# Moving the small transfers of row maxima from SyncE's transfer queue to ScalarE's, in a fused attention and gated-MLP block

## The chip, the cores and the metric

The kernel runs on one core of a Trainium2 chip. The time is that of one execution on the device in microseconds (us), and the median of three runs stands for the kernel. PE is TensorE, DVE is VectorE, ACT is ScalarE, POOL is GpSimd, SP is SyncE, which computes nothing and only starts transfers.

## The reference

S is 2048 rows, D is 512, there are 32 heads of 16 columns, and the gated MLP has 896 columns in each half.

```python
xn = layernorm(x)
q, k, v = split_heads(xn @ wqkv)                    # 32 heads of 16
p = softmax((q @ k.T) * 16 ** -0.5)                 # 2048 x 2048 for each head
attn = merge_heads(p @ v) @ wo
z = gelu(xn @ w_in)                                 # 2048 x 1792
z1, z2 = z[:, :896], layernorm(z[:, 896:])
mlp = (z1 * (w_sp @ z2 + b_sp[:, None])) @ w_out    # w_sp is 2048 x 2048
out = x + attn + mlp
```

## The kernel before

**Attention** sets the beat. Heads are taken in 16 pairs; a pair's queries are cut into 4 blocks of 512, so that there are 64 blocks, numbered here 0 to 63 in the order of work. A block has three kinds of work on PE. *Maxima* (`maxima`, L1237) are 16 steps of two matmuls that form raw scores with the queries on the partitions; DVE reduces each pair of PSUM banks to its row maxima (`max_red`, L826). *Scores* (`scores`, L1223) are 16 steps of two matmuls that form the scores again with the keys on the partitions, less the row's maximum, which takes part as two more rows of the stacked queries `qst` (rows 48 and 49 of 64, hence 50 rows in the profile's shapes). ACT takes the exponential of each step into a tile `pf` (L86, 128x1024). *Values* (`values`, L1324) multiply eight `pf` tiles at a time with the values, twice a block; the first half's sum is copied by ACT into `e`, the second is added to it by DVE (L1346).

**The row maxima have to travel.** They come out with the queries on the partitions and are needed as rows of `qst`. `max_fin` (L837 to L841) folds a block's maxima into `mrow`, one DVE transpose (L843) turns them into `ms`, one transfer *stores* `ms` in a small scratch tensor `mscr` in HBM (16 KB), and two transfers *load* it from there as the two rows of each head of the pair (`qst<-mscr`, 4 KB each). Scores of the block may stand on PE only from the planned time `maxready` on. Maxima are planned up to about 30 steps ahead of scores.

**Everything else is PE filler.** All projections, the spatial matmul `w_sp @ z2`, the output projections (`dense`, L1282) are cut into slots of two matmuls on half the rows each and are laid between the steps of attention by the pattern `ORDER`. Maxima, scores and values share three PSUM tiles `sl` of two banks; the filler has a pair of its own, `dps`. Weights and intermediate results travel by some 1350 transfers; the spatial weights `wsp` are split by POOL (L286 cast, L288 difference), the spatial inputs `zs` are loaded from `z2scr`.

**The order is written at build time by a planner** that keeps a clock for PE (`T["P"]`), ACT (`"A"`), DVE (`"D"`) and POOL (`"G"`). `spawn(generator, priority, ready)` puts a generator on its list; what it yields says on which engine the next piece runs and how long it is planned to take, `("T", us)` is a plain delay. `advance(t)` runs the pieces that are due. `after(us, move, ...)` puts a transfer on a list of times, and `flush()`, called once at each turn of the main loop, issues those that are due on SP's queue in order of time (`move`, L142, is SP's issue). Every queue then works in that order: an instruction that waits holds all that stand behind it on its engine, and no engine knows the planner's times.

**Eight counters.** A transfer from SP's or ACT's queue raises one of eight counters, named DMAHW0 to DMAHW7 in the program, and takes them in turn in the order in which the program was written, whichever of the two queues issues it. Before it may start, the transfer that used the same counter before, which is the eighth one before it, must have landed. That wait stands on the engine that issues the later transfer.

Of the kernel before, what the change touches and what calls it, by code (L numbers as in the profile page):

```python
# [68 lines left out]
def fused_block(ctx, tc, x, wqkv, wo, w_in, w_spT, b_sp, w_out, out):  # L69
    nc = tc.nc  # L70
# [11 lines left out]
    T = {"P": -1000.0, "A": 0.0, "D": 0.0, "G": -1000.0}  # L82
    ends = [0.0]
# [30 lines left out]
    qst = [cp.tile([P, S], F32R, name=f"qst{a}") for a in range(2)]  # L114
# [11 lines left out]
    mscr = [dr.tile([4, 32, 32], F32, name=f"mscr{i}") for i in range(4)]  # L126
# [11 lines left out]
    def raw(t):  # L138
        return t.bitcast(F32) if t.dtype == F32R else t
# [4 lines left out]
    def clock():  # L144
        return T["P"]
# [7 lines left out]
    def at(t, fn, *args):  # L153
        late.append((t, len(late), fn, args))
# [4 lines left out]
    def after(us, fn, *args):  # L159
        at(ends[0] + us, fn, *args)  # L160
# [26 lines left out]
    def queue_up(gen, prio, n, ready):  # L187
        want = next(gen, None)
        if want is not None:
            tasks.append((want[0], want[1], max([ready, *want[2:]]), prio, n, gen))  # L190

    def spawn(gen, prio=2, ready=None):
        count[0] += 1
        ends[0] = clock() if ready is None else ready
        queue_up(gen, prio, count[0], ends[0])
# [623 lines left out]
    maxready = {}  # L819

    def max_red(i, k, ready):
        g, (t, kc) = i // 16, divmod(i % 16, 4)
        yield "D", td(1024)
        if i % 16 == 0:
            mmax[g] = at_.tile([P, 2, 4, 4], F32, tag="mm", name=f"mm{g}", bufs=2)
        nc.vector.tensor_reduce(mmax[g][:, :, t, kc], sl[k], AX.X, ALU.max)  # L826
        free_slot(k)
        if i % 16 == 15:
            yield from max_fin(g)

    def max_fin(g):
        p, c = divmod(g, 4)
        yield "D", 0.95
        mm = mmax.pop(g)
        mn = at_.tile([P, 2, 4, 2], F32, tag="mn", name=f"mn{g}", bufs=1)
        mr = mrow[:, 0:16].rearrange("p (j a t) -> p j a t", j=2, a=2)
        nc.vector.tensor_reduce(mr[:, :, 0, :], mm, AX.X, ALU.max, negate=True)  # L837
        nc.vector.tensor_reduce(mn[:, :, :, 0], mm, AX.X, ALU.max, negate=True)
        nc.vector.tensor_reduce(mn.bitcast(F32R)[:, :, :, 1], mm, AX.X, ALU.max)
        with nc.allow_low_precision(reason="the second of two parts, of which the first is exact"):  # L840
            nc.vector.tensor_reduce(mr[:, :, 1, :], mn, AX.X, ALU.add)  # L841
        ms = at_.tile([P, 32], F32, tag="ms", name=f"ms{g}", bufs=2)
        nc.vector.transpose(ms, mrow.bitcast(F32))  # L843
        after(0.3, move, mscr[g % 4].rearrange("b k x -> (b k) x"), ms)
        for j in range(2):
            row = 64 * j + KS
            after(6.5 if g else 3.3, move, qst[p % 2][row:row + 2, c * 512:(c + 1) * 512].rearrange("a (t b x) -> a t b x", t=4, b=4), mscr[g % 4][:, 8 * j:8 * j + 8, :].rearrange("b (a t) x -> a t b x", a=2))
        maxready[g] = ends[0] + (12.0 if g else 8.5)

    def norm_out(g4, c):  # L850
        nh = 6 if g4 == 3 else 8
# [273 lines left out]
    with tc.manual_schedule(engines=engines):  # L1125
# [50 lines left out]
        stpos = {}  # L1176
        mode = "R"
        spawn(max_fin(0), 0, T["D"])
        n_st, n_mx, n_pv = 0, 16, 0

# [187 lines left out]
        while n_pv < N or queue or tasks or late or urgent or turn or slots:  # L1368
            t = T["P"]
# [74 lines left out]
```

## Time and profile before

| | |
|---|---|
| median of 3 runs | 1839.94 us (1839.93 to 1842.82) |
| the profiled execution, its span | 1837.59 us, 1835.7 us |
| PE, DVE, ACT, POOL busy | 98%, 79%, 66%, 37% of the span |
| granted TensorE clock | 0.998 |
| transfers of SP's queue | 53.0% of the 16 DMA engines' time |

The span is what the trace covers; the execution's own time is 1.9 us longer. A row of the timeline has start, duration, engine, line, operation, what is written and read, the number of instructions merged, and in brackets how long the engine was idle before and what ended that. A transfer's row shows its issue alone, on the queue of the engine that issues it (SPq), not when its data lands; a start is the time at which its waits were over. In the chain of work that ended last, a piece named DMA runs from a transfer's issue until its data landed.

### The profile page before, as it was taken

The page shows a single profiled execution, that of the slowest core. Times are in us where ns is not written, and L with a number is a line of the kernel's source. Part 1 is how long each engine was busy: PE and PEld are TensorE (multiplying, and loading weights), DVE is VectorE, ACT ScalarE, POOL GpSimd, SP SyncE. Part 2 cuts the span into 40 slices and gives each one's busy share as a digit, 9 for nine tenths or more (in the row PEclk, how much of TensorE's full clock was granted, in tenths as well). Part 3 has the DMA queues.
Part 4 walks back from the last instruction along what each step waited for, and adds up shares of the span by engine and source line. Part 5 has one row for each costly group of instructions (what it writes and reads, how often), then busy time and mean ns, then how long its engine had stood idle before and what let it go on. Part 6 is the DMA issues. An engine that isn't in the chain of part 4 may idle for free.

```text
span 1835.7 us, 38100 instructions
## 1 busy us (share of the span) xinstructions
PE 1800.9 (98%) x14744; PEld 1087.7 (59%) x14744; DVE 1443.6 (79%) x1695; ACT 1211.2 (66%) x1329; POOL 684.3 (37%) x786
## 2 busy tenths in 40 slices
PE   9999999999999999999999999999999999999998
PEld 7656566566556565565655655656566665656553
DVE  8858787888887787788877887778778877888882
ACT  4347777888877777566666665666666665666655
POOL 5451141677768677212532244103422140002201
PEclk9999999999999999999999999999999999999999
DMA  7866654433654236647757568655757477466422
GB/s 264 284 234 212 211 187 134 122 113 109 186 185 135 96 99 212 157 137 185 224 154 199 158 189 195 168 143 161 187 150 183 135 210 170 121 155 169 134 89 102
DMA packets 214911, 305.64 MB, mean 166 GB/s; under 512 B 37745, under 2 KB 107953, under 8 KB 214721
## 3 DMA queue, kind: packets, MB, share of 16 engines
q1 hardware_dynamic: 207240, 275.93, 53.0%
q0 software_dynamic: 7488, 27.27, 4.3%
q8 instruction: 116, 1.90, 0.5%
q14 instruction: 67, 0.54, 0.1%
HBM read 193.27 MB, written 109.85 MB: 165 GB/s over the span
## 4 chain that ended last, share of the span: by engine, by line
PE 91%; DVE 4%; DMA 2%; issue 1%; ACT 1%; SPq 1%; POOL 0%; DVEq 0%; POOLq 0%; ACTq 0%
PE dps L1282 36%; PE sl L1324 24%; PE sl L1223 14%; PE sl L1237 12%; DVE mm L826 4%; PE dps L1296 1%; SPq L142 1%; PE sl L247 1%; DMA zs<-z2scr 1%; PE sl L248 1%; PE sl L249 1%; ACT pf L86 0%; PE sl L970 0%; DMA wsp_14r<-in_w_spT 0%; PE sl L1039 0%
## 5 line engine op out<-in xcount | busy, mean ns | idle before, releaser
L826 DVE TENSOR_REDUCE mm<-sl 128x2 f32<-128x1024 f32 x1008 | 1208.7, 1222 | 187.7 <-PE sl L1237 178.8
L86 ACT ACTIVATE pf<-sl 128x1024 f32<-128x1024 f32 x1024 | 1042.9, 1026 | 329.0 <-PE sl L1223 292.4
L1324 PE MATMUL sl<-pf,vall 128*32 128x512 f32 x4096 | 467.9, 595 | 0.7 <-DVE on L960 0.7
L1223 PE MATMUL sl<-qst,kst 50*128 50x512 f32 x2048 | 435.0, 418 | 7.5 <-DVE mm L826 2.3
L1237 PE MATMUL sl<-kst,qst 48*128 48x512 f32 x2016 | 414.8, 404 | 3.9 <-DVE mm L826 2.6
L1282 PE MATMUL dps<-wsp,zs 64*128 64x512 f32 x2352 | 381.0, 392 | 2.2 <-DMA zs<-z2scr 1.4
L1223 PEld LDWEIGHTS sl<-qst,kst 50*128 50x128 f32 x2048 | 194.3, 184 | 221.0 <-issue 80.6
L1324 PEld LDWEIGHTS sl<-pf,vall 128*32 128x32 f32 x4096 | 119.2, 109 | 266.5 <-issue 235.0
L1237 PEld LDWEIGHTS sl<-kst,qst 48*128 48x128 f32 x2016 | 191.8, 185 | 104.5 <-ACT pf L86 49.4
L1282 PEld LDWEIGHTS dps<-wsp,zs 64*128 64x128 f32 x2352 | 227.6, 187 | 38.5 <-DMA zs<-z2scr 2.1
L86 ACT ACTIVATE e<-sl 128x512 f32<-128x512 f32 x64 | 38.3, 598 | 189.8 <-PE sl L1324 175.1
L1346 DVE TENSOR_TENSOR e<-sl,e 128x512 f32<-128x512 f32 x64 | 44.3, 692 | 130.1 <-PE sl L1324 85.5
L729 POOL TENSOR_TENSOR hhl<-z1i,hhl 128x512 fp32r<-128x512 f32 x28 | 35.9, 1292 | 281.1 <-ACT hhl L86 259.1
L1282 PE MATMUL dps<-w,xt 64*128 64x448 f32 x768 | 110.5, 368 | 1.7
L1282 PE MATMUL dps<-wout,hp 64*128 64x512 f32 x672 | 110.5, 392 | 0.1
L877 POOL TENSOR_TENSOR ob<-ob 128x512 f32<-128x512 f32 (+1 forms) x16 | 20.5, 1284 | 169.1 <-DMA ob<-rscr 151.5
L1282 PEld LDWEIGHTS dps<-w,xt 64*128 64x128 f32 x768 | 73.7, 186 | 16.1 <-issue 8.5
L1282 PEld LDWEIGHTS dps<-wout,hp 64*128 64x128 f32 x672 | 64.3, 187 | 10.2 <-issue 0.5
L397 POOL TENSOR_TENSOR qkhl<-qr,qkhl 128x512 fp32r<-128x512 f32 x24 | 30.4, 1284 | 102.3 <-ACT qkhl L86 92.4
L873 POOL TENSOR_TENSOR ob<-ob 128x512 f32<-128x512 f32 (+1 forms) x16 | 20.6, 1287 | 104.2 <-DMA ob<-escr 104.2
L1282 PE MATMUL dps<-wf,zs 64*128 64x512 f32 x336 | 55.6, 393 | 0.1
L1282 PE MATMUL dps<-xnT,wqk 64*128 64x512 f32 x288 | 48.0, 394 | 0.3
(292 smaller groups left out, 1693.1 us busy)
## 6 DMA issues: line engine op xcount, KB each, us to landing
zs<-z2scr SPq DMA_DIRECT2D x192, 256.0 KB
escr<-e SPq DMA_DIRECT2D x60, 256.0 KB
hscr<-hhl POOLq DMA_DIRECT2D x28, 512.0 KB, 6.0
qst<-qscr SPq DMA_DIRECT2D x60, 192.0 KB
kst<-kscr SPq DMA_DIRECT2D x60, 192.0 KB
qscr<-qkhl SPq DMA_DIRECT2D x16, 512.0 KB
kscr<-qkhl SPq DMA_DIRECT2D x16, 512.0 KB
xt<-xscr SPq DMA_DIRECT2D x64, 128.0 KB
```

The source lines that it names most:

```text
L86: return nc.scalar.activation(out, in_, func, **kw)
L142: nc.sync.dma_start(raw(dst), raw(src))
L397: nc.gpsimd.tensor_sub(hl[:, 1, :], raw_, hl[:, 0, :].bitcast(F32))
L729: nc.gpsimd.tensor_sub(hl[:, 1, :], z1, hl[:, 0, :].bitcast(F32))
L826: nc.vector.tensor_reduce(mmax[g][:, :, t, kc], sl[k], AX.X, ALU.max)
L873: nc.gpsimd.tensor_add(both_[rows, 0, :], both_[rows, 0, :], both_[rows, 1, :])
L877: nc.gpsimd.tensor_mul(both_[rows, 0, :], both_[rows, 0, :], both_[rows, 1, :])
L1223: nc.tensor.matmul(sl[k][:, j, :], kst[p % 2][rows, kt * P:(kt + 1) * P], qst[p % 2][rows, c * 512:(c + 1) * 512], start=True, stop=True)
L1237: nc.tensor.matmul(sl[k][:, j, :], qst[p % 2][rows, tt * P:(tt + 1) * P], kst[p % 2][rows, kc * 512:(kc + 1) * 512], start=True, stop=True)
L1282: nc.tensor.matmul(dps[:, bank, :w], lhs, rhs, start=go, stop=stop)
L1324: nc.tensor.matmul(sl[k][cols:cols + VW, 0, :], vpack(kt + r, 2 * p + j), pf[:, j * 512:(j + 1) * 512], start=n % CYC == 0, stop=n % CYC = ...
L1346: nc.vector.tensor_add(e, sl[k][:, 0, :], e)
```

## The change

The store and the two loads of each block go out on ACT's queue (`nc.scalar.dma_start`) in place of SP's, and they are planned otherwise. Before, all three were on the list of times: the store 0.3 us after the folding was planned to end, the loads 6.5 us after it (3.3 us for the first block). Now a new generator, `max_rows`, is spawned with priority 1, that of the exponentials: the store is an ACT piece of 0.15 us, the loads one ACT piece of 0.3 us, planned 4.5 us (2.5 us for the first block) after the store. `maxready` keeps its 12.0 us (8.5 us), counted from 0.1 us later, since `spawn` moves the time it is counted from. No arithmetic changes, and no wait for data: the store still waits for `ms`, the loads for the store's landing.

```diff
         nc.vector.transpose(ms, mrow.bitcast(F32))
-        after(0.3, move, mscr[g % 4].rearrange("b k x -> (b k) x"), ms)
+        spawn(max_rows(p, c, g, ms), 1, ends[0] + 0.1)
+        maxready[g] = ends[0] + (12.0 if g else 8.5)
+
+    def max_rows(p, c, g, ms):
+
+        yield "A", 0.15
+        nc.scalar.dma_start(mscr[g % 4].rearrange("b k x -> (b k) x"), ms)
+        yield "T", 4.5 if g else 2.5
+        yield "A", 0.3
         for j in range(2):
             row = 64 * j + KS
-            after(6.5 if g else 3.3, move, qst[p % 2][row:row + 2, c * 512:(c + 1) * 512].rearrange("a (t b x) -> a t b x", t=4, b=4), mscr[g % 4][:, 8 * j:8 * j + 8, :].rearrange("b (a t) x -> a t b x", a=2))
-        maxready[g] = ends[0] + (12.0 if g else 8.5)
+            nc.scalar.dma_start(raw(qst[p % 2][row:row + 2, c * 512:(c + 1) * 512].rearrange("a (t b x) -> a t b x", t=4, b=4)), mscr[g % 4][:, 8 * j:8 * j + 8, :].rearrange("b (a t) x -> a t b x", a=2))
```

**Where the instructions now stand.** Of the 192 transfers, 64 stores and 128 loads, all leave SP (1349 rows, now 1157) and come to ACT (1312, now 1504). Lines after L843 have numbers 7 higher in the changed kernel. The names in the rows below are tiles with a running number; the brackets name the counters and engines that a row waits for.

The first place is block 31, where the second quarter of the spatial weights is being loaded. SP's queue before:

```order
L142 DMA zs_10446<-z2scr 64x2x512 [waits DMAHW0_49]
L142 DMA mscr_166<-ms_10468 128x32 [waits DMAHW1_49,DVE_49]
L142 DMA wsp_14r<-in_w_spT 128x512 [waits DMAHW4_49,DMAHW2_49,Pool_49]
L142 DMA wsp_15r<-in_w_spT 128x512 [waits DMAHW3_49,PE_49]
L142 DMA qst_91<-mscr_166 2x16x32 [waits DMAHW1_49]
L142 DMA qst_91<-mscr_166 2x16x32 [waits DMAHW5_49]
L142 DMA zs_10586<-z2scr 64x2x512 [waits DMAHW6_49,DMAHW2_49,Pool_49]
L142 DMA zs_10586<-z2scr 64x2x512 [waits DMAHW7_49]
L142 DMA os_3_10492<-escr_3_134 128x1x32 [waits DMAHW0_49]
```

The counters run on by one from row to row, and the two loads stand ahead of the `zs` loads, which wait for POOL. The same place of SP's queue now:

```order
L142 DMA zs_10436<-z2scr 64x2x512 [waits DMAHW0_49]
L142 DMA wsp_14r<-in_w_spT 128x512 [waits DMAHW4_49,DMAHW1_49,Pool_49]
L142 DMA wsp_15r<-in_w_spT 128x512 [waits DMAHW6_49,DMAHW2_49,Pool_49]
L142 DMA zs_10575<-z2scr 64x2x512 [waits DMAHW3_49,DMAHW1_49,Pool_49]
L142 DMA zs_10575<-z2scr 64x2x512 [waits DMAHW5_49]
L142 DMA os_3_10482<-escr_3_134 128x1x32
L142 DMA os_3_10482<-escr_3_134 128x1x32 [waits DMAHW7_49]
L142 DMA ob_3_10483<-escr_3_134 128x1x512 [waits DMAHW0_49]
```

The three small transfers are gone; `wsp_15r` takes counter 2, the first `zs_10575` counter 3, and counter 4, which is skipped here, is the store's. ACT's queue at the same place now:

```order
L86 ACTIVATE pf_10432<-sl_201 128x1024 [waits DVE_49,PE_49]
L850 DMA mscr_166<-ms_10458 128x32 [waits DMAHW4_49,DVE_49]
L86 ACTIVATE e_2_10478<-sl_201 128x512 [waits PE_49]
L86 ACTIVATE pf_10489<-sl_202 128x1024 [waits PE_49,Activation_49]
L86 ACTIVATE pf_10505<-sl_201 128x1024 [waits PE_49,Activation_49]
L855 DMA qst_91<-mscr_166 2x16x32 [waits DMAHW4_49,DMAHW2_49]
L855 DMA qst_91<-mscr_166 2x16x32 [waits DMAHW3_49]
L86 ACTIVATE pf_10524<-sl_203 128x1024 [waits DVE_49,PE_49,Activation_49]
```

The store now stands ahead of the copy to `e`, the loads ahead of the third exponential after it; the first load waits for the store (counter 4) and for `wsp_15r` (counter 2), the second for the first `zs_10575` (counter 3).

The second place is block 61, in the output projection at the end. ACT's queue now:

```order
L86 ACTIVATE pf_19181<-sl_203 128x1024 [waits DVE_49,PE_49]
L850 DMA mscr_164<-ms_19202 128x32 [waits DMAHW1_49,DVE_49]
L86 ACTIVATE e_0_19221<-sl_203 128x512 [waits PE_49]
L86 ACTIVATE pf_19243<-sl_202 128x1024 [waits PE_49,Activation_49]
L86 ACTIVATE pf_19256<-sl_203 128x1024 [waits PE_49,Activation_49]
L855 DMA qst_91<-mscr_164 2x16x32 [waits DMAHW2_49,DMAHW1_49]
```

And SP's queue there now:

```order
L142 DMA op_0_19222<-oscr 64x2x128 [waits DMAHW7_49,PE_49]
L142 DMA op_0_19222<-oscr 64x2x128 [waits DMAHW0_49]
L142 DMA op_0_19222<-oscr 64x2x128
L142 DMA op_0_19222<-oscr 64x2x128 [waits DMAHW2_49]
L142 DMA op_1_19227<-oscr 64x2x128 [waits DMAHW3_49]
```

The third of these transfers takes counter 1 (its own earlier use is over by then), and it is this transfer that the store on ACT waits for; before, the store stood ahead of all of them, on SP.

PE's work is the same but for the dummy matmuls that the planner puts where it sees PE idle (`filler`, L1296): the changed program has ten fewer of them.

## The prediction

> **What bounds the kernel now.** I read the page's engine shares and its chain first.
>
> ```profile
> span 1835.7 us, 38100 instructions
> PE 1800.9 (98%) x14744; PEld 1087.7 (59%) x14744; DVE 1443.6 (79%) x1695; ACT 1211.2 (66%) x1329; POOL 684.3 (37%) x786
> PE 91%; DVE 4%; DMA 2%; issue 1%; ACT 1%; SPq 1%; POOL 0%; DVEq 0%; POOLq 0%; ACTq 0%
> ```
>
> PE is busy all but 34.8 us, so a change that leaves PE's work alone can gain little and can lose whatever makes PE wait. ACT has idle time, but the question is where. The second view is that of who waits: PE's waits for transfers, and SP's own waits.
>
> ```profile
> PE dps L1282 <- DMA zs<-z2scr: 1.4, 2, 0.7
> SPq L142 <- DVE ms L843: 252.8, 52, 10.7
> SPq L142 <- DMA mscr<-ms: 42.5, 16, 6.7
> ```
>
> The columns are total, times, longest. PE itself waits 1.4 us for `zs`. SP, where the three small transfers stand now, waits 252.8 us for `ms` and 42.5 us for a store to land, and nobody is hurt: SP computes nothing. The change moves these waits to ACT, and PE depends on ACT within a step or two. Two rows at 78 us show how closely:
>
> ```profile
> 77.46 1.02 ACT L86 ACTIVATE pf<-sl 128x1024 f32<-128x1024 f32 x1 [0.61 <-PE sl L1223]
> 78.38 0.59 ACT L86 ACTIVATE vall<-dps 128x512 f32<-128x512 f32 x1
> 79.08 1.02 ACT L86 ACTIVATE pf<-sl 128x1024 f32<-128x1024 f32 x1
> 78.54 0.50 PE L1223 MATMUL sl<-qst,kst 50*128 50x512 f32 x2 [0.66 <-ACT pf L86]
> ```
>
> One extra copy of 0.59 us on ACT among the exponentials, and PE stands idle for 0.66 us, since the PSUM tile that the late exponential reads is needed again. I therefore price time lost on ACT among the exponentials **one to one** on PE.
>
> **The ordinary block.** Block 19 as it runs now (DVE's transpose, SP's three issues, ACT beside them):
>
> ```profile
> 600.97 0.21 DVE L843 STREAM_TRANSPOSE ms<-mrow 128x32 f32<-128x32 f32 x1
> 601.21 0.32 SPq L142 DMA_DIRECT2D mscr<-ms  x1
> 604.63 1.27 SPq L142 DMA_DIRECT2D qst<-mscr  x2
> 602.62 0.60 ACT L86 ACTIVATE e<-sl 128x512 f32<-128x512 f32 x1 [2.16 <-PE sl L1324]
> 604.50 3.35 ACT L86 ACTIVATE pf<-sl 128x1024 f32<-128x1024 f32 x3 [0.36 <-PE sl L1223]
> ```
>
> The store falls into the 2.16 us in which ACT waits for the values before `e`: it costs **nothing** while its waits are over by then. If that cover is gone, `e` and all behind it are late by the rest. The loads go between two exponentials. These start every (3.35 - 1.03) / 2 = 1.16 us, since PE makes no more; the two issues take 1.27 us. Whether ACT can issue while it computes, no row of before shows, as ACT issues nothing. The two ends come from the nearest rows:
>
> ```profile
> 62.99 1.28 POOL L288 TENSOR_TENSOR wqk<-wqk_0r,wqk 128x512 fp32r<-128x512 f32 x1
> 64.23 0.58 POOL L1154 DMA_DIRECT2D xscr<-xnT  x1
> 64.81 0.62 POOL L286 CAST wqk<-wqk_1r 128x512 fp32r<-128x512 f32 x1
> 933.28 1.98 ACT L86 ACTIVATE pf<-sl 128x1024 f32<-128x1024 f32 x2 [0.37 <-PE sl L1223]
> ```
>
> POOL issues in line: its transfer starts when the operation before ends, and the next operation when the transfer's issue ends. On ACT that would be 1.03 + 1.27 - 1.16 = 1.14 us late a block, about 45 x 1.14 = 51 us over the 45 or so blocks without a wait of their own (below). ACT's own row points the other way: two exponentials of 1.03 us in 1.98 us, the second taken up before the first has ended. With the issue beside the computing it is 1.27 - 1.16 = 0.1 us a block, **5 us**. I take the 5, as the row is ACT's own, and keep 51 for the range; below 5 it can reach 0.
>
> [...]
>
> **What the loads and stores wait for.** This is the term that matters. Each of the 192 transfers now waits on ACT for the transfer eight before it in the program, mostly one of SP's. In most blocks that one has landed long before. With SP's and ACT's rows laid side by side for all 64 blocks, it has not in 18. For the time to land, three pieces of the chain serve (from issue to landing), and for the three blocks in which the spatial weights are split (31, 38, 45) these rows of SP, POOL and ACT:
>
> ```profile
> 1113.76 5.53 DMA wsp_14r<-in_w_spT
> 1126.88 9.97 DMA zs<-z2scr
> 1724.67 4.60 DMA escr<-e
> 932.41 1.27 SPq L142 DMA_DIRECT2D zs<-z2scr  x2
> 931.10 1.29 POOL L288 TENSOR_TENSOR wsp<-wsp_14r,wsp 128x512 fp32r<-128x512 f32 x1
> 928.37 3.35 ACT L86 ACTIVATE pf<-sl 128x1024 f32<-128x1024 f32 x3 [0.34 <-PE sl L1223]
> 1121.42 1.29 SPq L142 DMA_DIRECT2D zs<-z2scr  x2
> 1116.55 3.35 ACT L86 ACTIVATE pf<-sl 128x1024 f32<-128x1024 f32 x3 [0.37 <-PE sl L1223]
> 1307.35 1.23 SPq L142 DMA_DIRECT2D zs<-z2scr  x2
> 1307.02 3.35 ACT L86 ACTIVATE pf<-sl 128x1024 f32<-128x1024 f32 x3 [0.37 <-PE sl L1223]
> ```
>
> In block 31 the first `zs` starts when POOL has split `wsp_14` (931.10 + 1.29). With 4.6 us, the least of the three pieces, it lands at 937.0, the second load's issue ends at 937.6, and the exponential behind it, now at 928.37 + 1.16 = 929.5, is 8.1 us late. POOL sets this, so it doesn't go away when SP runs ahead. Block 38 has the first load behind the same `zs`: 1121.4 + 4.6 + 1.3 - 1117.7 = 9.6. Block 45: 1307.35 + 4.6 + 0.64 - 1308.2 = 4.4. Together 22 us; SP's weights and so POOL start a little earlier in 38, as SP doesn't wait for `ms` there, so I count **20**.
>
> Bursts of SP's transfers just ahead of the loads come next; block 33 is the plainest:
>
> ```profile
> 978.92 2.03 SPq L142 DMA_DIRECT2D ob<-escr  x2
> 990.89 1.36 SPq L142 DMA_DIRECT2D qst<-mscr  x2
> 983.04 3.36 ACT L86 ACTIVATE pf<-sl 128x1024 f32<-128x1024 f32 x3 [0.34 <-PE sl L1223]
> ```
>
> The second `ob` starts about 979.5, the load waits for it, and the exponential behind the loads starts at 984.2. Landed at the earliest (4.6 us) that is 0.6 us late, landed when SP could go on (990.9) 7.3; I take 5. Blocks 6, 7, 17, 22, 23 and 49 are of this kind and smaller, 1 to 3 us each where the same rows are laid side by side. As SP, no longer held by `ms`, starts some of these bursts earlier, I count **14** for the seven.
>
> The last stretch has eight transfers in a row, and the store waits for the third of them in block 61:
>
> ```profile
> 1732.96 5.31 SPq L142 DMA_DIRECT2D op<-oscr  x8
> 1734.93 2.62 DMA op<-oscr
> 1733.79 0.60 ACT L86 ACTIVATE e<-sl 128x512 f32<-128x512 f32 x1 [3.76 <-PE sl L1324]
> ```
>
> The third starts at 1732.96 + 2 x 0.66 = 1734.3 and lands 2.6 us later, at 1736.9; the store's issue then ends 3.5 us after `e` is due. Blocks 54, 55, 56, 59, 60 and 62 have the same at the loads, by 1 to 5 us; I count **15** for the seven. The last of the 18 is block 1:
>
> ```profile
> 102.55 0.74 SPq L142 DMA_DIRECT2D wsp_1r<-in_w_spT  x1
> 93.84 1.03 ACT L86 ACTIVATE pf<-sl 128x1024 f32<-128x1024 f32 x1
> ```
>
> The loads come after `wsp_1r` in the program. As SP runs now that would be 102.55 + 5.53 + 0.64 - 93.84 = 14.9 us; but SP stood 10.7 us for `ms` just before (its longest such wait) and will be ahead by much of it, so **6**, between 0 and 15.
>
> **What is gained.** SP is free of 64 x (0.32 + 1.27) us of issue and of both waits, and its queue runs earlier; PE's 1.4 us of waiting for `zs` is what that can return. Ten dummy matmuls fewer are worth 1.4 us:
>
> ```profile
> 1827.71 1.42 PE L1296 MATMUL dps<-brow,zeror 64*128 64x512 f32 x10
> ```
>
> [...]
>
> **Sum.** 20 + 14 + 15 + 6 = 55 for the waits, + 5 for the issues, - 1.4 = 58.6 us on 1837.59 of the profiled execution, 1896.2. That execution lies 2.35 us under the median of the runs, so against the median it is 1839.94 + 58.6 = 1898.5; I say **1898**.
>
> **Rivals.**
>
> - *Issue in line:* as the forecast, but ACT issues as POOL does: 46 us more, **1944**. For it: POOL's rows. Against: ACT takes up work before the last has ended.
> - *ACT stands behind SP's issues too:* where SP issues in a burst, in the 18 blocks above, each load also waits for one of SP's issues to end, 1.27 / 2 = 0.63 us by the `zs` rows: 18 x 2 x 0.63 = 23 us more, **1921**. For it: nothing in this trace; against: two queues, as far as it shows. [...]
> - *The waits melt:* SP, rid of 252.8 us of waiting, keeps so far ahead that only the three blocks which POOL holds remain: 20 + 5 - 1.4, some 24 us, **1863**. Against: most bursts start from PE's or POOL's own progress.
> - *It doesn't matter:* each eighth transfer before has landed when ACT comes, the issues vanish beside the exponentials: **1840**. Block 31 speaks against it.
> - *Faster:* ACT's queue is where the maxima are short of wait, and SP's bulk transfers start earlier by up to 10.7 us a block. Its place is the chain's DMA and SPq, 3% or 55 us, but PE's own waits cap it: 1.4 us for `zs`, the ten dummies 1.4, and at most some 5 more at weight loads that hide behind them, **1832**. It decides if ACT's waits sum to less than those 8 us.
>
> **How the numbers follow.** Forecast 0.48, in line 0.20, behind SP's issues 0.05, melting 0.12, no matter 0.06, faster 0.09. The range reaches from the low side of melting, 1850 (below it block 31 would have to fail too), to 1955 (in line, with 11 us more, which the upper ends of blocks 1 and 33 make: 9 and 2); outside lie the last two cases and tails. About 0.2%, 3.7 us, is what a measurement of this kernel can tell from no change. Faster by more: 0.09; within: 0.06; slower: 0.85.
>
> **What would show it.** Transfers of `mscr` on ACT's queue, with idle ACT before them that ends with `zs`, `ob`, `op` or `wsp_1r`; in blocks 31, 38 and 61 a gap of 3 to 10 us on ACT and PE together; ACT's exponentials 1.16 us apart around the loads elsewhere (right) or 2.3 us apart (in line). PE's busy time nearly as before, its idle time up by 50 to 60 us. I am wrong if the blocks named show no gap, if gaps on ACT leave PE busy, or if the time went where no transfer of `mscr` stands.

## The result, and the profile after

The changed kernel takes **1939.28 us** (median of four runs, 1936.15 to 1944.42) against 1841.10 us (1839.93 to 1842.82) for the kernel before: a ratio of 1.0539, 95% interval 1.0518 to 1.0561. The prediction said slower, 1898 us, with a range of 1850 to 1955. The sign and the range held; the loss is 98 us where the forecast had 58.6.

The profiled execution took 1936.15 us. These lines of its page answer to those shown of before: the span, the engines, the granted clock in 40 slices, the chain.

```profile
span 1934.2 us, 38083 instructions
PE 1833.0 (95%) x14734; PEld 1101.3 (57%) x14734; DVE 1443.2 (75%) x1695; ACT 1209.4 (63%) x1329; POOL 684.9 (35%) x786
PEclk9989999999999999999999998999999999999999
PE 72%; DMA 10%; DVE 6%; POOL 3%; issue 3%; ACT 2%; ACTq 1%; SPq 1%; DVEq 0%; POOLq 0%
```

The span grew by 98.5 us. PE's idle time went from 34.8 to 101.2 us, 66.4 more; but its busy time grew as well, by 32.1 us, with ten matmuls fewer. Two causes are to be found, then, and the two eights in the row of the clock point to the second. In the chain transfers have 10% in place of 2%.

The view of waits (total, times, longest) says who stood for whom:

```profile
PE sl L1244 <- ACT pf L86: 69.1, 31, 11.4
ACT pf L86 <- DMA qst<-mscr: 51.5, 33, 12.3
ACT pf L86 <- DMA zs<-z2scr: 10.9, 2, 7.2
ACT pf L86 <- DMA wsp_1r<-in_w_spT: 9.7, 1, 9.7
ACT e L86 <- DMA mscr<-ms: 7.2, 3, 4.2
```

PE waits for exponentials, and the exponentials wait for what stands ahead of them in ACT's queue. Block 31 shows it row by row, on the timeline of the changed kernel (ACT's rows, then SP's, POOL's and PE's):

```profile
963.52 1.03 ACT L86 ACTIVATE pf<-sl 128x1024 f32<-128x1024 f32 x1 [0.33 <-PE sl L1230]
968.41 3.20 ACTq L855 DMA_DIRECT2D qst<-mscr  x2
971.73 1.94 ACT L86 ACTIVATE pf<-sl 128x1024 f32<-128x1024 f32 x2 [7.18 <-DMA zs<-z2scr]
...
965.52 0.33 SPq L142 DMA_DIRECT2D wsp_15r<-in_w_spT  x1
967.41 1.24 SPq L142 DMA_DIRECT2D zs<-z2scr  x2
...
966.13 1.26 POOL L288 TENSOR_TENSOR wsp<-wsp_14r,wsp 128x512 fp32r<-128x512 f32 x1
...
972.81 0.80 PE L1244 MATMUL sl<-kst,qst 48*128 48x512 f32 x2 [6.53 <-ACT pf L86]
973.40 0.63 PE L1289 MATMUL dps<-wsp,zs 64*128 64x512 f32 x2
```

The first load waits for `wsp_15r`, starts at 968.41, and the second waits for the first `zs`, which SP could start only at 967.41, when POOL's split of `wsp_14` had ended (966.13 + 1.26). ACT idles 7.18 us, PE 6.53. And PE's matmuls, once they run again, are slow: two in 0.63 us where two took 0.40 before the stop (two of the same kind at 956.68 us). In the view of stretches around that stop a row has the stretch, its length, then the busy time of PE, PEld (PE's weight loads), DVE, ACT and POOL with the number of instructions in brackets, and last the granted clock, the DMA engines' busy share and GB/s; so the clock is the third number from the end:

```profile
965.90:972.80 6.90, 0.38 (x4) 0.00 (x0) 0.54 (x1) 1.07 (x2) 3.28 (x4) 0.85 0.60 154
972.80:977.50 4.70, 4.69 (x22) 3.76 (x24) 2.45 (x2) 2.34 (x3) 0.00 (x0) 0.50 0.83 161
977.50:985.00 7.50, 7.18 (x60) 2.96 (x58) 3.74 (x4) 3.64 (x5) 1.28 (x1) 1.00 0.08 20
```

For 4.7 us after the stop PE runs at 0.50 of its clock: 22 matmuls, where the stretch behind it does 60 in 7.5. The trace's clock records hold 12 such stretches in the body of the execution (20 us from its start to 20 us from its end), each of 3.41, 6.83 or 10.24 us, 71.7 us together. The kernel before has none there. Of the 71.7 us, 21.2 lie within PE's idle time. If all of PE's work in the rest took twice its time, they cost (71.7 - 21.2) / 2 = **25.3 us**; this is an estimate.

Blocks without such a wait cost nothing. Block 19, as shown of before, but from the changed kernel:

```profile
623.05 0.32 ACTq L850 DMA_DIRECT2D mscr<-ms  x1
626.35 2.18 ACT L86 ACTIVATE pf<-sl 128x1024 f32<-128x1024 f32 x2 [0.37 <-PE sl L1230]
627.58 1.27 ACTq L855 DMA_DIRECT2D qst<-mscr  x2
628.96 1.02 ACT L86 ACTIVATE pf<-sl 128x1024 f32<-128x1024 f32 x1 [0.42 <-PE sl L1230]
```

The loads' issue begins at 627.58 while an exponential runs until 628.53, and the next one stands 0.42 us idle where 0.36 was usual. The next block's store follows 27.20 us later (650.25); before, the two stores stood 27.16 apart.

### The profile page after: what moved, and what is told of

It is laid out like the page before. It is cut to its first block, busy times and chain, and to the rows that moved or that the text cites. A ratio compares the mean times of both kernels' runs of the same rounds, so it can differ in the third digit from the quotient of the medians.

```text
span 1934.2 us, 38083 instructions
## 1 busy us (share of the span) xinstructions
PE 1833.0 (95%) x14734; PEld 1101.3 (57%) x14734; DVE 1443.2 (75%) x1695; ACT 1209.4 (63%) x1329; POOL 684.9 (35%) x786
## 4 chain that ended last, share of the span: by engine, by line
PE 72%; DMA 10%; DVE 6%; POOL 3%; issue 3%; ACT 2%; ACTq 1%; SPq 1%; DVEq 0%; POOLq 0%
PE dps L1289 28%; PE sl L1331 19%; PE sl L1230 11%; PE sl L1244 11%; DVE mm L826 4%; DMA mscr<-ms 3%; ACT pf L86 2%; DMA zs<-z2scr 2%; POOL wsp L288 1%; ACTq L855 1%; DMA hp<-hscr 1%; SPq L142 1%; PE dps L1303 1%; POOL wsp L286 1%; PE sl L247 0%
## 5 line engine op out<-in xcount | busy, mean ns | idle before, releaser
L1244 PE MATMUL sl<-kst,qst 48*128 48x512 f32 x2016 | 425.4, 415 | 72.4 <-ACT pf L86 69.1
L1289 PE MATMUL dps<-wsp,zs 64*128 64x512 f32 x2352 | 386.8, 398 | 0.0
L1289 PEld LDWEIGHTS dps<-wsp,zs 64*128 64x128 f32 x2352 | 232.1, 190 | 36.5
```

The costliest lines, as they stand in the source:

```text
L1244: nc.tensor.matmul(sl[k][:, j, :], qst[p % 2][rows, tt * P:(tt + 1) * P], kst[p % 2][rows, kc * 512:(kc + 1) * 512], start=True, stop=True)
L1289: nc.tensor.matmul(dps[:, bank, :w], lhs, rhs, start=go, stop=stop)
```

## The experiments

The theory after this comparison: **(a)** ACT stands, at the head of its queue, for a transfer to land, either the eighth before (the counter) or the block's own store, and PE for ACT; **(b)** a long stop of PE costs more than its length, since the granted clock is then halved. Rivals: the issues themselves; the other planned order; a stop costs just its length. Ten kernels, each timed beside runs of the kernel before (medians 1838.33 to 1839.98 us), which the ratios go by:

| kernel | us (median) | ratio, 95% | PE idle | half clock |
|---|---|---|---|---|
| before (profile above) | 1841.10 | | 34.8 | 0 |
| changed | 1939.28 | 1.0518 to 1.0561 | 101.2 | 71.7 |
| sp_order | 1840.54 | 0.9996 to 1.0020 | 35.4 | 3.4 |
| store_act | 1846.30 | 1.0024 to 1.0049 | 38.1 | 6.8 |
| loads_act | 1891.40 | 1.0252 to 1.0314 | 66.5 | 44.4 |
| loads_late | 1890.97 | 1.0255 to 1.0305 | 73.8 | 34.1 |
| no_store_wait | 1915.26 | 1.0405 to 1.0436 | 85.1 | 68.3 |
| store_sp | 1867.63 | 1.0131 to 1.0176 | 49.9 | 13.7 |
| loads_act_late | 1891.41 | 1.0249 to 1.0319 | 70.5 | 34.1 |
| pad_long | 1927.03 | 1.0465 to 1.0497 | 99.3 | 81.9 |
| pad_mid | 1926.24 | 1.0455 to 1.0491 | 85.3 | 75.1 |
| pad_short | 1882.02 | 1.0219 to 1.0253 | 67.8 | 0 |

PE's idle time is span less busy time of each page; half clock is the sum of the clock records at 0.50, counted as above.

### The queue, or the order that goes with it?

`sp_order` is the changed kernel with both issues given back to SP, every planned time kept.

```diff
-        nc.scalar.dma_start(mscr[g % 4].rearrange("b k x -> (b k) x"), ms)
+        nc.sync.dma_start(mscr[g % 4].rearrange("b k x -> (b k) x"), ms)
...
-            nc.scalar.dma_start(raw(qst[p % 2][row:row + 2, ...
+            nc.sync.dma_start(raw(qst[p % 2][row:row + 2, ...
```

> The changed kernel with its planned order kept to the row, only the three transfers issued by SP again. Theory (ACT, at the head of its queue, waits for an earlier transfer to land, PE stands idle for it, and the granted clock is halved for some us after the longer stops): 1838 to 1844 us, PE's idle time back at about 35 us, no stretch at half clock between 20 and 1830 us. Rival 'planned order' (other times of the transfers and the maxima, not the queue): about 1939 us, as the changed kernel.

Measured: 1840.54 us, no different from before. The whole loss belongs to the queue; the planned order by itself costs nothing. One condition of the theory failed: one stretch of half clock, 3.4 us from 1137.2 us on, stands in this run too, behind a stop of 1.06 us in block 38 in which PE waited for `zs` itself. With its 1.7 us it is no part of the loss.

### The store alone, the loads alone

In `store_act` only the store is on ACT, the loads are on SP's list of times as before; in `loads_act` the store is on that list, and the generator issues only the loads (the second diff).

```diff
-        yield "T", 4.5 if g else 2.5
-        yield "A", 0.3
         for j in range(2):
             row = 64 * j + KS
-            nc.scalar.dma_start(raw(qst[p % 2][row:row + 2, ...
+            after(6.5 if g else 3.3, move, qst[p % 2][row:row + 2, ...
```

```diff
-        yield "A", 0.15
-        nc.scalar.dma_start(mscr[g % 4].rearrange("b k x -> (b k) x"), ms)
-        yield "T", 4.5 if g else 2.5
+        after(0.3, move, mscr[g % 4].rearrange("b k x -> (b k) x"), ms)
+        yield "T", 4.65 if g else 2.65
```

> Only the store goes out on ACT, the two loads stay on SP as before. Theory (waits of the loads): 1838 to 1848 us, since the store waited on ACT for 7.2 us in all in the changed kernel, in 3 places. Rival 'issue' (each transfer that ACT issues costs its engine time): a third of the transfers, so about 1841 + 98/3 = 1874 us by count, or 1841 + 98/5 = 1861 by issue time (0.32 of 1.59 us).

> Only the two loads go out on ACT, the store stays on SP. Theory (waits of the loads): nearly the whole loss stays, 1920 to 1950 us, and a little more than the changed kernel is possible because SP's queue, with the store in it, again stands for the maxima. Rival 'issue': two thirds to four fifths of 98 us, 1906 to 1920 us. Rival 'the store on ACT is what hurts': about 1841 us.

The store alone: 1846.30, within what the theory said, and some 7 us over the kernel before. Its largest stop of PE, 2.61 us, is in block 61, where the store waits for `op`; another of 2.27 us, in block 38, is PE's own wait for `zs`. The loads alone: 1891.40, some 29 us less than expected. The loads carry most of the loss, but it isn't a fixed toll: the stops of blocks 1, 31, 38 and 45 were gone, those of 29, 33 and 49 were there (4.5, 5.3 and 4.0 us of PE). Where the store stands thus decides what the loads wait for. The next pair takes that up.

### Why the place of the store matters

`store_sp` is the changed kernel with one word changed, `nc.scalar` to `nc.sync` at the store. The counters are given out in the order of the built program, in which the builder lays the two queues into one another; that order shifts when SP has the store and stands for the maxima.

> The changed kernel with one word changed: the store goes out on SP's queue, the loads stay on ACT. The order of the work on PE, DVE and POOL, and of ACT's computing, is that of the changed kernel to the row. But the builder lays the two queues into one another anew: with SP standing for the maxima, the loads' eighth transfer before is an older one in blocks 30, 31, 37, 38 and 45 (in 31 two of the spatial weights in place of the held zs). Theory 'eighth before': the gaps of those five blocks and of block 1 go, 9.0 + 1.5 + 6.5 + 1.6 + 11.4 + 3.0 = 33 us, and about 13 us of half clock; near the kernel with the loads alone on ACT: 1893 us, between 1880 and 1905. Rival 'planned order': the loads alone were cheaper because their planned times differed; then 1939 us, as the changed kernel.

Measured: 1867.63 us, below the expected band. All six named stops went, as the theory said, but others went too that it had not named: 33, 49 and 53 don't stop either, and 29 only for 0.9 us. Block 31 of this kernel (ACT, then SP):

```profile
940.41 1.25 ACTq L855 DMA_DIRECT2D qst<-mscr  x2
941.78 1.94 ACT L86 ACTIVATE pf<-sl 128x1024 f32<-128x1024 f32 x2 [0.42 <-DMA qst<-mscr]
...
936.22 0.33 SPq L850 DMA_DIRECT2D mscr<-ms  x1
936.65 0.37 SPq L142 DMA_DIRECT2D wsp_14r<-in_w_spT  x1
937.12 0.38 SPq L142 DMA_DIRECT2D wsp_15r<-in_w_spT  x1
944.33 1.24 SPq L142 DMA_DIRECT2D zs<-z2scr  x2
```

The same loads, the same held `zs` on SP (944.33), but now the eighth before is `wsp_13r` and `wsp_14r`, and ACT's idle time is the ordinary 0.42 us instead of 7.18. Blocks 6, 7 and 62 still stop (3.4, 2.0 and 4.3 us of PE). This kernel and `loads_act` issue the same transfers from the same queues; only their planned times and order differ, and they lie 24 us apart. So the order, free of cost on SP, matters once ACT issues the loads. The prediction counted it as relief that SP, rid of the maxima, runs ahead. In block 31 of these two kernels it is the other way round: the more of SP's transfers stand ahead of the loads in the built order, the younger is the eighth before them.

### The block's own store

In the chain of the changed kernel, the pieces over 5 us that run from a store's issue to its landing:

```profile
785.82 7.12 DMA mscr<-ms
816.99 5.83 DMA mscr<-ms
899.09 7.42 DMA mscr<-ms
1025.36 7.91 DMA mscr<-ms
1261.87 6.54 DMA mscr<-ms
1485.19 6.90 DMA mscr<-ms
1568.87 5.63 DMA mscr<-ms
1596.22 8.18 DMA mscr<-ms
```

These are blocks 25, 26, 29, 33, 41, 49, 52 and 53: up to 8.2 us for 16 KB, where the loads of an ordinary block stand 4.2 to 5.2 us behind their store and need not wait. `no_store_wait` takes that wait away with other data.

```diff
+    mzero = dr.tile([4, 32, 32], F32, name="mzero")
+    nc.gpsimd.dma_start(mzero.rearrange("b k x -> (b k) x"), zeror[:, 0:32].bitcast(F32))
...
-                ... mscr[g % 4][:, 8 * j:8 * j + 8, :].rearrange("b (a t) x -> a t b x", a=2))
+                ... mzero[:, 8 * j:8 * j + 8, :].rearrange("b (a t) x -> a t b x", a=2))
```

> The changed kernel, but the two loads read a constant tensor of zeros in place of the block's own maxima, which are still stored; so the loads wait for the eighth transfer before them and no longer for their own store. The scores are then formed without their maxima. Theory 'own store' (the store's 16 KB stand behind bulk transfers in the DMA engines): the gaps of blocks 25, 26, 29, 33, 41, 49, 52, 53 and 60 go, 24 us of PE's idle time, and the half clock after them, 30.7 us of records, 15 us: about 1900 us, between 1890 and 1915; those of blocks 1, 7, 31, 38 and 45 stay. Rival 'counters only' (the eighth before is what is late everywhere): all gaps stay, 1939 us.

Measured: 1915.26, just outside the band. The stops of 25, 26, 29, 41 and 52 went; 33, 49, 53 and 60 stayed at 3.7, 2.0, 2.7 and 2.4 us (and 1, 7, 31, 38 and 45, as expected, at 3.1 to 9.8 us), since there a late eighth before (`ob`, `qst<-qscr`, the store itself by its counter, `op`) stands beside the own store. Block 41, first as changed, then without the wait; the idle time before the exponential falls from 2.80 us to the ordinary 0.39:

```profile
1268.43 1.28 ACTq L855 DMA_DIRECT2D qst<-mscr  x2
1269.84 1.94 ACT L86 ACTIVATE pf<-sl 128x1024 f32<-128x1024 f32 x2 [2.80 <-DMA qst<-mscr]
```

```profile
1249.82 1.27 ACTq L857 DMA_DIRECT2D qst<-mzero  x2
1251.22 1.94 ACT L86 ACTIVATE pf<-sl 128x1024 f32<-128x1024 f32 x2 [0.39 <-DMA qst<-mzero]
```

### Would planning the loads later help?

`loads_late` is the changed kernel, `loads_act_late` the one with the loads alone on ACT, each with the loads planned 3 us later.

```diff
-        yield "T", 4.5 if g else 2.5
+        yield "T", 7.5 if g else 2.5
...
-        yield "T", 4.65 if g else 2.65
+        yield "T", 7.65 if g else 2.65
```

> The changed kernel with the loads planned 7.5 us after the store in place of 4.5 (block 0 as it was), the time from which scores may stand unchanged. Theory (waits for landings): each gap is up to 3 us shorter; of the eight gaps over 3 us some 23 us stay (9.2, 3.8, 3.2, 6.7, 5.8, 11.6, 3.2, 3.8 less 3.0 each), the shorter ones go, and half clock falls from 72 to about 27 us: 1841 + 23 + 13 = 1877 us, between 1860 and 1895. Rivals 'issue' and 'planned order': no change, 1939 us. Rival 'late maxima' (scores then wait for the rows instead): above 1939 us, with PE idle before the first scores of each block.

> The kernel with the loads alone on ACT, these planned 3 us later (7.65 in place of 4.65 us after the maxima). Theory (waits for landings, dearer through the clock): its gaps of 4.5, 5.3, 4.0, 3.6 and 3.5 us (blocks 29, 33, 49, 60, 62) become 1.5, 2.3, 1.0, 0.6 and 0.5 us, the shorter ones go, and the half clock with them: 1840 + 6 + 4 = 1850 us, between 1840 and 1862. Rival 'a stall of fixed size for each load that ACT issues': 1891 us, as with the loads early. Rival 'late maxima': scores wait for the rows, over 1862 us.

`loads_late`, 1890.97, came out within the theory's range: half the loss is gone, the own stores have landed, and the long stops of blocks 1, 31 and 38 remain (7.8, 4.1, 9.3 us). Block 53 still stops too (4.2 us), now for an `hp` load that is the eighth before. `loads_act_late`, 1891.41, did not: no gain at all. Four old stops are gone or small (block 29 none, 33 and 49 0.9 us, 60 none), that of 62 stayed (3.6 us), and new ones stand in 37, 53 and 57 (4.7, 3.3, 4.0 us), for a load that is planned later comes behind other transfers of SP, and its eighth before is another one. Block 37 there:

```profile
1112.03 5.37 ACTq L854 DMA_DIRECT2D qst<-mscr  x2
1117.50 1.94 ACT L86 ACTIVATE pf<-sl 128x1024 f32<-128x1024 f32 x2 [5.39 <-DMA wsp_3r<-in_w_spT]
...
1109.44 0.33 SPq L142 DMA_DIRECT2D wsp_3r<-in_w_spT  x1
```

So neither rival of that run holds as it was put: it isn't a toll per load, and late maxima are a small part (PE waits 3.6 us for `qst` in all). My expectation failed because it took the neighbours as given.

### What a stop costs: three lengths, the same work

Three versions of the kernel before, all transfers on SP. Each adds 250 copies of 64 columns on ACT at the place of the loads, of which the planner knows nothing; only their grouping differs. The diff is that of `pad_long`; `pad_mid` has 10 copies in every second block, `pad_short` 5 in every block.

```diff
+        if g % 5 == 2 and 10 <= g < 60:
+            spawn(pads(25), 1, ends[0] + 0.1)
...
+    def pads(n):
+        yield "T", 4.65
+        yield "A", 0.01
+        for _ in range(n):
+            act(pad, pad, AF.Copy)
```

> The kernel before (all transfers on SP), with 25 small copies on ACT, about 0.23 us each by the two copies that the traces show, at the place of the loads, in 10 blocks (12, 17, ... 57): 10 stops of some 5.8 us, 58 us of ACT in all, which the planner does not know of. Theory 'clock' (a stop of this length halves the granted clock for 3.4 to 10 us): PE idle 10 x 5.4 = 54 us more, and about 10 x 6.8 us of half clock, 34 us: 1840 + 88 = 1928 us, between 1905 and 1935. Rival 'one to one' (a stop costs its own length): 1840 + 54 = 1894 us.

> The same 250 copies, 10 in each of 25 blocks (every second one from 10): 25 stops of some 2.3 us. Theory 'clock': PE idle about 25 x 2.0 = 50 us more; the changed kernel had 3.4 us of half clock after some of its gaps of 1.5 to 2.5 us and none after others, so by half of them 25 x 0.5 x 1.7 = 21 us: 1840 + 71 = 1911 us, between 1890 and 1925. Rival 'one to one': 1890 us, as the other two.

> The same 250 copies, 5 in each of 50 blocks (10 to 59): 50 stops of some 1.15 us. Theory 'clock': no half clock, PE idle 50 x 0.8 = 40 us more: 1880 us, between 1860 and 1895, so 30 us or more under the long stops though ACT does the same work. Rival 'one to one': as the long stops, about 1890 us.

Measured: 1927.03, 1926.24 and 1882.02 us. The same 250 copies of 0.256 us cost 89, 88 and 44 us: 8.9 us a stop of PE of 6.2 to 6.5 us, 3.5 us one of about 2.1, 0.9 us one of at most 0.8. "One to one" falls, and the stops of middle length were dearer than I had put them (expected up to 1925). The clock is not all of the difference. PE's idle time grew by 64.5, 50.5 and 33.0 us, since a short loss on ACT is covered in part in every block (the copies take 64 us of ACT in each of the three kernels); half clock, counted as above, adds some 25, 37 and 0 us. The stretches around one stop of `pad_long`, and around one of `pad_mid`:

```profile
564.80:571.00 6.20, 0.04 (x2) 0.04 (x2) 0.05 (x1) 5.63 (x21) 5.92 (x7) 0.86 0.90 241
571.00:576.00 5.00, 5.00 (x24) 3.97 (x26) 2.45 (x2) 2.21 (x3) 0.00 (x0) 0.50 0.02 4
576.00:581.00 5.00, 5.00 (x46) 1.88 (x44) 1.86 (x3) 3.21 (x5) 1.20 (x3) 1.00 0.01 3
```

```profile
1168.90:1171.10 2.20, 0.01 (x2) 0.00 (x0) 0.41 (x1) 2.07 (x7) 1.67 (x2) 1.00 1.05 309
1171.10:1172.50 1.40, 1.39 (x12) 1.17 (x14) 0.78 (x1) 1.01 (x2) 0.78 (x2) 1.00 1.02 263
1172.50:1175.90 3.40, 3.40 (x20) 2.65 (x18) 1.99 (x3) 1.91 (x2) 1.31 (x2) 0.50 0.99 197
```

24 matmuls in 5 us against 46. After 2.20 us of standing still the clock even runs on in full for 1.4 us and is halved then. `pad_short` has no half clock at all, and a stop of it looks so (ACT, then PE):

```profile
1226.99 1.40 ACT L86 ACTIVATE pad<-pad 128x64 f32<-128x64 f32 x5
1228.30 1.92 ACT L86 ACTIVATE pf<-sl 128x1024 f32<-128x1024 f32 x2
...
1229.36 0.50 PE L1247 MATMUL sl<-kst,qst 48*128 48x512 f32 x2 [0.76 <-ACT pf L86]
```

Its PE is busy 11.5 us longer than before (1812.4 against 1800.9) without half clock, 0.23 us for each of 50 stops: in the row above two matmuls after the stop take 0.50 us, where 0.40 is usual. I call this the restart, but it isn't settled: by the same account `pad_mid` and `pad_long` have nothing left for it (PE busy 36.7 and 23.5 us longer, of which half clock is put at 37 and 25).

## Why the prediction was right, and short by 41 us

The prediction's terms, beside PE's stops of 0.8 us and more in the same blocks of the changed kernel:

| term | predicted | measured |
|---|---|---|
| blocks 31, 38, 45, held by POOL | 20 | 6.5 + 11.4 + 3.0 = 21.0 |
| bursts: 6, 7, 17, 22, 23, 33, 49 | 14 | 1.5 + 3.6 + 0 + 0 + 1.3 + 5.6 + 2.5 = 14.5 |
| last stretch: 54, 55, 56, 59, 60, 61, 62 | 15 | 0.9 + 1.2 + 2.3 (54, 55, 60) = 4.4 |
| block 1 | 6 | 9.0 |
| blocks not named: 25, 26, 29, 30, 37, 41, 52, 53 | 0 | 16.5 |
| issues beside computing | 5 | about 0 |
| dummies | -1.4 | -1.4 |
| half clock | 0 | 25.3 |
| not accounted for (restarts, small stops) | 0 | the rest, 9 |

- **What bounds, and where the waits would stand:** right. The gaps came in 31 and 38 (6.5 and 11.4 us of PE), and `store_sp` shows that it was the eighth before. In block 61 the store did hold up ACT, but PE had no stop of 0.8 us there.
- **The issues:** right in kind, nothing in size. Block 19 shows the issue beside the exponential, so *issue in line* falls, although its 1944 lies near the measured time. *ACT behind SP's issues* falls too: the least, median and longest issue of a load (ns, from the view of the tile `mscr`) leave no room for it in most blocks. In the 18 blocks that the rival is about every one took 0.60 to 0.64 us, and of the 41 loads that began while an issue of SP was under way, 39 did.
```profile
L855 ACTq DMA_DIRECT2D qst<-mscr x128: 603/626/1191, 67.2 to 1888.5; - x128
```

- **"Each of the 192 transfers now waits on ACT for the transfer eight before it in the program", late in 18 blocks:** incomplete. The loads also wait for their own store, and the sum took it as landed. The row for this stood in the prediction: SP waited 42.5 us for `mscr`, 16 times, up to 6.7 us. I read it as harmless on SP and didn't carry it over to ACT. Six of the eight blocks not named are of this kind (13.5 us; 30 and 37, 3.0 us, wait for `wsp_5r`), and so are parts of the stops in 33 and 49 (5.6 and 2.5 us, and 3.7 and 2.0 without that wait).
- **The last stretch** was over-priced by 11 us: what ACT lost there PE mostly didn't feel.
- **"I therefore price time lost on ACT among the exponentials one to one on PE":** this is the step that failed. The row behind it was a stop of 0.66 us, and it was misread: PE stood from 77.88 to 78.54 us, but the extra copy starts only at 78.38 us, behind the exponential that PE was waiting for. So that row showed no price for time lost on ACT. At that length the price holds all the same (`pad_short`: 0.9 us a stop). For stops of 2 us and more it doesn't (`pad_mid`, `pad_long`). The 25.3 us of half clock, for which the sum has no term, are most of the 41 us. PE's busy time, forecast as nearly unchanged, grew by 32.1 us. Without half clock and the rest of 9 the terms sum to 64, near the 58.6, but that is luck in part: 16.5 us were left out and 15.6 priced too high (the last stretch and the issues).
- *The waits melt*, *it doesn't matter* and *faster* fall: SP running ahead moved waits onto the loads.

What stays open: what the 9 us are, why PE rode over ACT's loss in the last stretch, and why the stores of eight blocks landed so late.

## What to carry to other kernels

Before a transfer goes to the queue of a computing engine, list everything that its issue waits for (its data, the landing of what it reads, and the older transfer whose counter it takes, whichever queue that went out on), because the engine stands for the last of them, as ACT stood 7.18 us in block 31 for a `zs` load of SP's. Price a stop of TensorE by its length and by the clock. In the three padded kernels it cost, under a microsecond, about its length, from 2 us up its length and some 1.4 to 2.5 us more (3.5 for 2.1, 8.9 for 6.4). A small change of order can move such waits a long way (72 us between the changed kernel and `store_sp`), so a forecast from the present neighbours has a wide range.

## What the runs showed of the hardware

- **The clock after a stop.** In the profiles of the kernel before and of the changed one (20 us at each end left out) the records show half clock, begun within the stop or up to 1.2 us after its end, at none of 16 stops of PE of 0.5 to 1 us, at 1 of 12 of 1 to 2 us, at 3 of 4 of 2 to 3 us, and at all 8 longer ones. The length alone doesn't tell, then. Two stops of the changed kernel, of 2.15 and of 2.50 us, each with a stretch that comes behind it:

```profile
1268.77:1270.92 2.15, 0.00 (x0) 0.00 (x1) 0.16 (x1) 1.08 (x2) 0.00 (x0) 1.00 0.29 66
1271.11:1274.52 3.41, 3.41 (x18) 2.63 (x18) 1.93 (x2) 1.70 (x2) 0.00 (x0) 0.50 0.36 92
...
1492.05:1494.55 2.50, 0.00 (x1) 0.00 (x0) 0.17 (x1) 1.07 (x2) 0.00 (x0) 1.00 1.04 322
1494.55:1498.00 3.45, 3.45 (x30) 2.72 (x32) 2.40 (x2) 2.91 (x3) 0.00 (x0) 1.00 0.78 281
```

  Behind the shorter stop PE does 18 matmuls in 3.41 us, behind the longer one 30 in 3.45. What decides between them was not shown.
- **An issue on ACT runs beside ACT's computing**, 0.32 us for the store and 0.63 for a load: in block 19 of the changed kernel the loads' issue began at 627.58 us, under an exponential that ran until 628.53. Its wait doesn't: it holds all that follows, in block 31 for 7.18 us of ACT's idle time.
- **A queue of its own didn't make these transfers fast.** The two queues of the changed kernel, SP's and ACT's (packets, MB, share of the 16 engines' time):

```profile
q1 hardware_dynamic: 193672, 274.35, 50.3%
q10 hardware_dynamic: 13568, 1.58, 0.6%
```

  ACT's queue is nearly empty, yet its 16 KB stores took from issue to landing up to 8.18 us. No run here shows what made these stores late. The DMA engines were 63% busy or more in the eight stretches of the late stores; but they were 94% busy or more in the 5 us after the stores of blocks 54 and 56 to 59 too, and those blocks' first loads, 4.2 to 4.3 us behind, didn't wait.
